# Attention read and rational feed-forward on one core: batch 0's softmax by token halves, early transfers in buffers of the units, and a new list

## The chip, the core and the metric

One core of a Trainium2 chip: TensorE (PE), VectorE (DVE), ScalarE (ACT), GpSimd (POOL), and SyncE (SP), which here issues every DMA. The metric is device microseconds of one execution; lower is better.

## The reference, cut to what matters

Eight batches of eight heads, 512 tokens x and 32 state rows, 64 columns a head.

```python
scores = scale * x @ state.T            # per batch and head
a = softmax(scores, axis=-1)            # "row" softmax, over the 32 states
xread = a @ state
a2 = softmax(scale * state @ x.T, -1)   # "column" softmax, over the 512 tokens
sread = a2 @ x
X = concat([xread, sread], axis=2)      # (B, H, 544, 64) -> rows of 512 = H * D
h = X @ w_in                            # 512 -> 2048
P = a0 + a1*h + a2*h**2 + a3*h**3
Q = 1 + |b0|*|h| + |b1|*h**2
out = (P / (Q + 1e-6)) @ w_out          # 2048 -> 512
```

## The kernel before

**Units.** The hidden width 2048 is cut into U = 8 slices of 256. A unit n is a slice of one batch: n = 8 * batch + slice, 64 units for the token rows; units 64 to 71 do the state reads of all batches. For the token rows `a @ state @ w_in` is regrouped: the products state @ w_in (`extra`, L601, token `X:i` with i = 4 * slice + e; each covers two batches) are made once, in the first 120 us, and are the weights of each unit's first layer. Products of batch 0 are split at once into a high and a low part (`fh` ACT, `fo` DVE); the rest is copied out of PSUM (`XA` by ACT, `XV` by DVE) into a tile `xo` (L618, two buffers), stored to DRAM (`XS`, L624), and loaded and split again later (`lm`, `fs`).

**A unit.** First layer `F:n:0`, `F:n:1` (L696, six matmuls each: high by high, high by low and low by high of the two halves), into a PSUM tile with tag `h`, of which there are two; products, the later batches' scores and transpositions use the same two. Then ACT makes C (`FC`, L708) and A (`FB`, L715) from it; DVE makes three steps that read it, `mu`, `po` on C (L719, L723) and `qd` on A (L729), after which the PSUM buffer is free; ACT `qa`, `ln`, `ex` (a reciprocal through logarithm and exponential, tile L); DVE `g1` (high part of the result, tile gh), `g2`, `g3`; POOL `gl` (low part, tile gl, L759). Second layer `mh:n:t` (four matmuls) and `ml:n:t` (two) for four token tiles t (L769), summed over the eight units of a batch in four PSUM banks, then copied and stored (`fl`/`fv`, `fd`). C and A have three buffers each, L, gh and gl two.

**Weights.** They come as 64-bit words and are converted: a pair k of raw halves is loaded (`lr:2k`, `lr:2k+1`, 512 KB each, L271, tile `raw`, two buffers of two halves); ACT makes one part (`cp`, L294), DVE another (`jr`, L304, "conversion" below), and DVE joins them (`jl`, L320): for input weights into `win_sb` (three buffers, stored by `jw` for later), for output weights into a tile that ACT and POOL split into `wo` (`sp`, L331, L332).

**Batch 0's attention** (L394 to L569). Scores by token halves g (L402), two heads' halves j in two PSUM banks. Row softmax for each j: transposition of blocks of 32 (`row_T`, DVE, L441), maxima (L458), subtraction (L466), exponential (ACT, L490), sums (L494), reciprocal (L500, L501), normalization (L507), transposition back (`a_T`, L513), high part (`a_hi`, ACT, L518), low part (`a_lo`, L522). The first layer of batch 0's units needs the high and low parts of both j. Column softmax: scores copied to SBUF by ACT (`sc_copy`, L412), maximum (`col_max`, DVE, L416) and `col_scale`, exponential with sum (`col_exp`, ACT, L447), transposition by PE (`e2_T`), then the state read (`sread`, L540). Suffixes choose the engine: `row_sub`, `a_lo`, `row_norv` run on DVE, `row_sup`, `a_lp`, `row_norm` on POOL.

**Order.** `ORDER` (L23) is one list of some 2,200 tokens, written out; each token is one call of a function, and each engine runs its instructions in the order of the list. A SyncE transfer that waits for a buffer or for data holds every later one.

```python
    ps_h = ctx.enter_context(tc.tile_pool(name="ps_h", bufs=2, space=PSUM))
    with tc.manual_schedule():
        for name, args in tokens:
            ops[name](*args)
```

Of the kernel before, what the change touches and what calls it, by code (L numbers as in the profile page):

```python
# [9 lines left out]
F32 = mybir.dt.float32  # L10
F32R = mybir.dt.float32r
I32 = mybir.dt.int32
U32 = mybir.dt.uint32
# [5 lines left out]
P = 128  # L19
# [169 lines left out]
def attention_rational_ffn(  # L189
# [7 lines left out]
    nc = tc.nc  # L197
# [10 lines left out]
    CW = DF // U  # L208
# [51 lines left out]
    for u in range(U):  # L260
        groups.append(("out", u))
        if u + 3 < U:
            groups.append(("in", u + 3))
    NU = 2 * len(groups)
    RAW, CV, win_t = {}, {}, {}

    def unit(i):
# [676 lines left out]
```

## Time and profile before

| what | us |
|---|---|
| median of 3 runs (668.93 to 676.08) | 672.35 |
| the profiled execution's own time | 671.54 |
| its span, first to last instruction | 669.7 |
| PE busy | 643.5 |
| DVE busy | 624.2 |
| ACT busy | 515.8 |
| POOL busy | 318.3 |

The span and the busy times are of one profiled execution; what lies around the span is 1.84 us. A busy time counts instructions on the engine, not the queue's waits. Starts are counted from the first instruction.

### The profile page before, as it was taken

Reading aid. Unit: us, or ns where it says so; the run is one execution under the profiler, and the core shown is the slowest. Engines: PE = TensorE matmul, PEld = TensorE weight load, DVE = VectorE, ACT = ScalarE, POOL = GpSimd, SP = SyncE. Lnnn points to the kernel's source line nnn. Section 1 sums busy time; section 2 is a strip of 40 time slices with the busy share of each in tenths; the row PEclk is TensorE's granted clock in tenths of the full one; section 3 lists DMA queues with packets and bytes.
Section 4 is the critical chain, followed back from the end, with each engine's and each line's share of the span. In section 5 each row is a group of like instructions: output and inputs, shape, how many; then the busy total and the mean of one; then the engine's idle time right before and its main releaser. Section 6 shows DMA issues by size and latency. Waiting matters only on the chain.

```text
span 669.7 us, 11219 instructions
## 1 busy us (share of the span) xinstructions
PE 643.5 (96%) x4474; PEld 512.9 (77%) x4474; DVE 624.2 (93%) x593; ACT 515.8 (77%) x611; POOL 318.3 (48%) x172
## 2 busy tenths in 40 slices
PE   6769989999999999999999999999999999999997
PEld 3445556778887888788887888788878888888995
DVE  5889999999999999999999999999999899999885
ACT  4689898887877887787868787797787678865663
POOL 1105255355454566545554545555446446465541
PEclk8989999999999999999999999999999999999999
DMA  7889987615112422213223132231225101211301
GB/s 298 310 315 335 331 329 257 226 54 178 44 34 93 136 77 96 69 26 105 85 101 120 71 89 69 79 142 32 95 79 174 32 1 47 64 47 60 100 1 63
DMA packets 28984, 81.46 MB, mean 122 GB/s; under 512 B 2820, under 2 KB 2948, under 8 KB 28932
## 3 DMA queue, kind: packets, MB, share of 16 engines
q1 hardware_dynamic: 28932, 80.75, 35.1%
q8 instruction: 35, 0.57, 0.3%
q14 instruction: 17, 0.14, 0.1%
HBM read 52.95 MB, written 27.79 MB: 121 GB/s over the span
## 4 chain that ended last, share of the span: by engine, by line
PE 88%; DMA 5%; ACT 3%; DVE 2%; issue 1%; SPq 1%; ACTq 0%
PE h L696 28%; DMA m_dram<-xo 3%; PE ps_x L607 3%; PE o__5754 L769 2%; PE o__3525 L769 2%; PE o__1763 L769 2%; PE o__2310 L769 2%; PE o__4679 L769 2%; PE o__4049 L769 2%; PE o__2879 L769 2%; PE o__3495 L769 2%; PE o__5233 L769 2%; PE o__2341 L769 2%; PE o__5794 L769 2%; PE o__4054 L769 2%; PE o__5172 L769 2%
## 5 line engine op out<-in xcount | busy, mean ns | idle before, releaser
L759 POOL TENSOR_TENSOR gl<-C,L 128x1024 fp32r<-128x1024 f32 (+1 forms) x70 | 174.1, 2487 | 230.4 <-DVE C L752 174.0
L696 PE MATMUL h<-aT,m 128*128 128x512 f32 x768 | 191.3, 396 | 4.2 <-DVE xo L619 4.1
L696 PEld LDWEIGHTS h<-aT,m 128*128 128x128 f32 x768 | 144.9, 190 | 38.5 <-issue 3.5
L708 ACT ACTIVATE C<-h,cst 128x1024 f32<-128x1024 f32 (+1 forms) x72 | 83.3, 1157 | 44.6 <-PE h L696 32.1
L656 POOL TENSOR_TENSOR m<-m_sb,m 128x512 fp32r<-128x512 f32 x56 | 79.9, 1432 | 60.3 <-ACT m L655 40.0
L715 ACT ACTIVATE A<-h,cst 128x1024 f32<-128x1024 f32 (+1 forms) x72 | 76.7, 1066 | 29.2 <-PE h L696 26.9
L740 DVE SCALAR_TENSOR_TENSOR gh<-C,cst,L 128x1024 fp32r<-128x1024 f32 (+1 forms) x72 | 91.8, 1274 | 6.2 <-ACT L L811 2.6
L729 DVE SCALAR_TENSOR_TENSOR A<-A,b0a,h 128x1024 f32<-128x1024 f32 (+1 forms) x72 | 87.5, 1216 | 9.4 <-ACT A L715 7.2
L752 DVE SCALAR_TENSOR_TENSOR C<-C,cst,A 128x1024 f32<-128x1024 f32 (+1 forms) x72 | 88.8, 1233 | 2.2
L723 DVE SCALAR_TENSOR_TENSOR C<-C,cst,h 128x1024 f32<-128x1024 f32 (+1 forms) x72 | 87.8, 1219 | 2.1
L746 DVE SCALAR_TENSOR_TENSOR A<-A,gh 128x1024 f32<-128x1024 f32 (+1 forms) x72 | 88.0, 1222 | 1.6
L735 ACT ACTIVATE A<-A 128x1024 f32<-128x1024 f32 (+1 forms) x72 | 72.7, 1012 | 19.2 <-DVE A L729 19.1
L719 DVE TENSOR_TENSOR C<-C,h 128x1024 f32<-128x1024 f32 (+1 forms) x72 | 82.9, 1152 | 3.9 <-ACT C L708 2.4
L801 ACT ACTIVATE L<-A 128x1024 f32<-128x1024 f32 (+1 forms) x72 | 73.0, 1013 | 3.4 <-POOL gl L759 0.3
L811 ACT ACTIVATE L<-L 128x1024 f32<-128x1024 f32 (+1 forms) x72 | 72.9, 1014 | 1.5
L607 PE MATMUL ps_x<-win_sb,st 64*32 64x256 f32 x1024 | 36.3, 403 | 15.2 <-DVE win_sb L320 6.3
L607 PEld LDWEIGHTS ps_x<-win_sb,st 64*32 64x32 f32 x1024 | 17.8, 111 | 30.9 <-ACT xo L619 10.5
L655 ACT CAST m<-m_sb 128x512 fp32r<-128x512 f32 x56 | 33.9, 614 | 0.0
L619 ACT COPY xo<-ps_x 128x1024 f32<-128x1024 f32 (+1 forms) x26 | 23.8, 933 | 5.0 <-PE ps_x L607 2.8
L332 POOL TENSOR_TENSOR wo<-cv_r,wo 128x1024 fp32r<-128x1024 f32 x7 | 16.9, 2410 | 17.6 <-ACT wo L331 17.6
L696 PEld LDWEIGHTS h<-sh,m 128*128 128x128 f32 x192 | 24.2, 191 | 0.7
L696 PE MATMUL h<-sh,m 128*128 128x256 f32 x192 | 24.4, 283 | 0.0
(254 smaller groups left out, 1113.2 us busy)
## 6 DMA issues: line engine op xcount, KB each, us to landing
m_sb<-m_dram SPq DMA_DIRECT2D x28, 512.0 KB, 4.5
m_dram<-xo SPq DMA_DIRECT2D x24, 512.0 KB, 4.2
out_dram<-o_sb SPq DMA_DIRECT2D x34, 256.0 KB, 4.3
xT_sb<-in_xT_dram SPq DMA_DIRECT2D x16, 512.0 KB, 5.1
raw<-in_w_in_dram SPq DMA_DIRECT2D x16, 512.0 KB, 6.4
raw<-in_w_out_dram SPq DMA_DIRECT2D x16, 512.0 KB, 5.6
x_sb<-in_x_dram SPq DMA_DIRECT2D x16, 512.0 KB, 7.0
w_in_dram<-win_sb SPq DMA_DIRECT2D x8, 512.0 KB, 5.4
```

The lines of the kernel that those rows point to most:

```text
L656: nc.gpsimd.tensor_tensor(m[:, 1], t, m[:, 0].bitcast(F32), op=ALU.subtract)
L696: nc.tensor.matmul(h[:, ci * W : (ci + 1) * W], l, r, start=(q == 0), stop=(q == len(seq) - 1),)
L708: nc.scalar.activation(e["C"], e["h"], AF.Identity, scale=cst[:, 3:4], bias=cst[:, 2:3])
L715: nc.scalar.activation(e["A"], e["h"], AF.Abs, scale=cst[:, 5:6])
L719: nc.vector.tensor_tensor(e["C"], e["C"], e["h"], op=ALU.mult)
L723: nc.vector.scalar_tensor_tensor(e["C"], e["C"], cst[:, 1:2], e["h"], op0=ALU.add, op1=ALU.mult)
L729: nc.vector.scalar_tensor_tensor(e["A"], e["A"], b0a, e["h"], op0=ALU.add, op1=ALU.mult)
L740: nc.vector.scalar_tensor_tensor(e["gh"], e["C"], cst[:, 0:1], e["L"], op0=ALU.add, op1=ALU.mult)
L746: nc.vector.scalar_tensor_tensor(e["A"], e["A"], 1.0 + 1e-6, e["gh"].bitcast(F32), op0=ALU.add, op1=ALU.mult)
L752: nc.vector.scalar_tensor_tensor(e["C"], e["C"], cst[:, 0:1], e["A"], op0=ALU.add, op1=ALU.subtract)
L759: eng.tensor_tensor(e["gl"], e["C"], e["L"], op=ALU.mult)
L769: nc.tensor.matmul(O[t], e[l][:, j * W + t * P : j * W + (t + 1) * P], wo[:, k, 2 * u + j, :], start=(place == FIRST[n // U, t] and i + j ...
```

## The change

1. Row softmax of batch 0 by token halves: `row_T:0:j` takes the 256 tokens of half j from both PSUM banks (two instructions of 128x256), and `a_hi`, `a_lo` write that half of the tokens.
2. Column softmax of batch 0 reads the scores in PSUM; its two `sc_copy` are gone.
3. The raw halves of pairs k = 2, 3 and 4 go to one buffer each of gl, gh and L, tiles of the units that are first written later.
4. The copies of products 0 to 2 go to C buffers, of 3 to 5 to A buffers.
5. In the list: `row_sup` for `row_sub` and `row_norm` for `row_norv` in batch 0, `a_lp` for `a_lo` in batches 0 and 1, `row_sup` for `row_sub` in batch 1, `row_norm:7:0` for `row_norv:7:0`, `gl:69` for `gv:69`; `cp` and `jr` of pairs 2 to 4 by halves; `XV:2`, `XV:26`, `XV:30` for the ACT copies and `XA:4`, `XA:20`, `XA:27` for the DVE ones; the eight warm-up matmuls stand behind the scores; the first stores stand behind ten raw loads; the rest is ordered anew throughout.

```diff
 ORDER = [
-    "warm:8 lt:0:0 ls:0:2 lt:0:1 scores:0:0 lc scores:0:1 cb b0a row_T:0:0 row_max:0:0 row_sub:0:0 lr:1 "
-    "lr:0 cp:0:1 ls:2:8 lr:2 jr:0:1 sc_copy:0:0 cp:0:0 jr:0:0 jl:0 X:0 lr:3 sc_copy:0:1 col_max:0:1 "
-    "col_scale:0:1 row_exp:0:0 row_sum:0:0 row_eps:0:0 cp:1:0 lr:6 XA:0 row_norm:0:0 row_T:0:1 "
-    "row_max:0:1 row_sup:0:1 lr:7 XS:0 fh:0 fo:0 a_T:0:0 X:3 col_exp:0:1 XA:3 X:1 cp:1:1 X:2 "
-    "col_max:0:0 XA:1 XS:3 jr:1:0 jr:1:1 jl:1 X:5 row_exp:0:1 a_hi:0:0 col_scale:0:0 col_exp:0:0 XA:2 "
-    "row_sum:0:1 row_eps:0:1 row_norv:0:1 XS:1 lr:5 lr:4 XS:2 a_T:0:1 a_hi:0:1 a_lp:0:1 a_lo:0:0 lq:0:0 "
...
+    "lt:0:0 ls:0:2 scores:0:0 lt:0:1 row_T:0:0 row_max:0:0 scores:0:1 row_T:0:1 row_sup:0:0 warm:8 "
+    "col_max:0:0 lr:0 cp:0:0 col_scale:0:0 row_max:0:1 lr:1 row_exp:0:0 row_sum:0:0 cp:0:1 row_sup:0:1 "
+    "row_exp:0:1 col_max:0:1 col_scale:0:1 lr:2 cp:1:0 jr:0:1 col_exp:0:0 col_exp:0:1 jr:0:0 jl:0 "
+    "jr:1:0 row_eps:0:0 row_norm:0:0 lc lr:3 cp:1:1 ls:2:8 X:3 lr:7 lr:4 XA:3 X:0 fh:0 jr:1:1 XA:0 X:1 "
+    "row_sum:0:1 row_eps:0:1 row_norm:0:1 lr:8 jl:1 fo:0 lr:6 a_T:0:0 cp:2:0 XA:1 e2_T:0:0 X:5 a_T:0:1 "
+    "a_hi:0:0 a_lp:0:0 lr:5 col_eps:0 cb a_hi:0:1 cp:3:1 cp:3:0 XV:5 lr:11 a_lp:0:1 cp:2:1 b0a XS:0 X:2 "
+    "XV:2 X:4 XA:4 fh:1 jr:2:1 F:0:0 e2_copy:0:0 jr:2:0 jl:2 XS:3 F:0:1 XS:1 cp:4:0 FC:0 fo:1 XS:5 "
+    "F:1:0 jr:4:0 FB:0 jr:3:1 jr:3:0 jl:3 sp:3 qd:0 F:1:1 FC:1 FB:1 mu:0 po:0 qa:0 XS:4 lr:10 ln:0 lr:9 "
+    "cp:4:1 e2_T:0:1 mu:1 po:1 X:8 XA:8 qd:1 fh:2 ex:0 fo:2 XS:2 lq:0:1 jr:4:1 jw:0 jl:4 e2_copy:0:1 "
...
@@ -261,7 +262,13 @@
         groups.append(("out", u))
         if u + 3 < U:
             groups.append(("in", u + 3))
-    NU = 2 * len(groups)
+    EARLY = {2: "gl", 3: "gh", 4: "L"}
+    XEARLY = {0: "C", 1: "C", 2: "C", 3: "A", 4: "A", 5: "A"}
+    BUFS = {"C": 3, "A": 3, "L": 2, "gh": 2, "gl": 2}
+
+    def spare(tag, dtype):
+        return ew.tile([P, 2 * S], dtype, name="spare", tag=tag, bufs=BUFS[tag])
+
     RAW, CV, win_t = {}, {}, {}
 
     def unit(i):
@@ -270,9 +277,13 @@
 
     def load_raw(i):
         what, u, j = unit(i)
-        if i // 2 not in RAW:
-            RAW[i // 2] = cv.tile([P, 2, 2 * CW, 2], U32, name="raw", tag="raw", bufs=2)
-        r = RAW[i // 2][:, j]
+        k = i // 2
+        if k in EARLY:
+            RAW[k, j] = spare(EARLY[k], U32).rearrange("p (f w) -> p f w", w=2)
+        elif (k, 0) not in RAW:
+            t = cv.tile([P, 2, 2 * CW, 2], U32, name="raw", tag="raw", bufs=2)
+            RAW[k, 0], RAW[k, 1], RAW[k, None] = t[:, 0], t[:, 1], t
+        r = RAW[k, j]
         if what == "in":
             nc.sync.dma_start(
                 r.rearrange("p f w -> p (f w)"),
@@ -284,6 +295,11 @@
                 r, w_out[f * P : (f + 1) * P, :].rearrange("p (c w) -> p c w", w=2)
             )
 
+    def raw_words(k, j, w):
+        if j is None:
+            return RAW[k, None][:, :, :, w]
+        return RAW[k, j][:, :, w].unsqueeze(1)
+
     def conv_parts(k, j=None):
         if k not in CV:
             CV[k] = [
@@ -293,7 +309,7 @@
         js = slice(0, 2) if j is None else slice(j, j + 1)
         nc.scalar.activation(
             CV[k][0][:, js].bitcast(F32),
-            RAW[k][:, js, :, 1].bitcast(F32),
+            raw_words(k, j, 1).bitcast(F32),
             AF.Prelu,
             scale=2.0**-112,
             alpha=2.0**32,
@@ -303,7 +319,7 @@
         js = slice(0, 2) if j is None else slice(j, j + 1)
         nc.vector.tensor_scalar(
             CV[k][1][:, js],
-            RAW[k][:, js, :, 0],
+            raw_words(k, j, 0),
             2.0**-29,
             7.0,
             op0=ALU.mult,
@@ -415,7 +431,7 @@
         cm = once(b, "cm", at_tile("cm", [P, 2], 2))
         nc.vector.tensor_reduce(
             cm if j is None else cm[:, j : j + 1],
-            half(TS[b]["sT"], j),
+            half(TS[b].get("sT", TS[b]["ps"]), j),
             axis=AX.X,
             op=ALU.max,
         )
@@ -437,8 +453,14 @@
 
     def row_T(b, j=None):
         e1 = once(b, "e1", at_tile("e1", [P, 2, S]))
-        for i in (0, 1) if b == 0 and j is None else (j,):
-            nc.vector.transpose(flat(half(e1, i)), flat(half(TS[b]["ps"], i)))
+        if b:
+            nc.vector.transpose(flat(e1), flat(TS[b]["ps"]))
+            return
+        w = S // 2
+        for i in range(2):
+            nc.vector.transpose(
+                e1[:, j, i * w : (i + 1) * w], half(TS[b]["ps"], i)[:, j * w : (j + 1) * w]
+            )
 
     def col_exp(b, j):
         T = TS[b]
@@ -446,7 +468,7 @@
         r2 = once(b, "r2", at_tile("r2", [P, 2], 2))
         nc.scalar.activation(
             e2[:, j],
-            T["sT"][:, j],
+            half(T.get("sT", T["ps"]), j),
             AF.Exp,
             scale=SCALE,
             bias=T["cm"][:, j : j + 1],
@@ -512,17 +534,27 @@
         t = once(b, "eT", lambda: at.tile([P, 2, S], F32, name="eT", tag="e2" if b else "e2T"))
         nc.vector.transpose(flat(half(t, j)), flat(half(TS[b]["e1"], j)))
 
+    def halves(b, t, j):
+        if b:
+            return half(t, j)
+        w = S // 2
+        return t[:, :, j * w : (j + 1) * w]
+
+    def turned(b, j):
+        t = half(TS[b]["eT"], j)
+        return t if b else t.rearrange("p (j t) -> p j t", j=2)
+
     def a_hi(b, j=None, copy=None):
         if b not in AT:
             AT[b] = at.tile([P, 2, 2, S], F32R, name="aT", tag="aT", bufs=2)
-        (copy or nc.scalar.copy)(half(AT[b][:, 0], j), half(TS[b]["eT"], j))
+        (copy or nc.scalar.copy)(halves(b, AT[b][:, 0], j), turned(b, j))
 
     def a_lo(b, j=None, eng=None):
         a = AT[b]
         (eng or nc.vector).tensor_tensor(
-            half(a[:, 1], j),
-            half(TS[b]["eT"], j),
-            half(a[:, 0].bitcast(F32), j),
+            halves(b, a[:, 1], j),
+            turned(b, j),
+            halves(b, a[:, 0].bitcast(F32), j),
             op=ALU.subtract,
         )
 
@@ -615,7 +647,11 @@
     def extra_out(i, copy):
         u, e = divmod(i, B // 2)
         q0 = 1 if e == 0 else 0
-        t = XO[i] = ew.tile([P, 2, 2, CW], F32, name="xo", tag="xo", bufs=2)
+        if i in XEARLY:
+            t = spare(XEARLY[i], F32).rearrange("p (q j f) -> p q j f", q=2, j=2)
+        else:
+            t = ew.tile([P, 2, 2, CW], F32, name="xo", tag="xo", bufs=2)
+        XO[i] = t
         copy(t[:, q0:].rearrange("p q j f -> p j q f"), XP[i][:, :, q0:])
 
     def extra_store(i):
```

## Rows read from the trace of the kernel before

**Rows 1.** The page: the span, the busy time of each engine with its share of the span and its instructions, and of the 40 equal slices those of PE and of the DMA engines (tenths; a slice is 16.7 us).

```profile
span 669.7 us, 11219 instructions
...
PE 643.5 (96%) x4474; PEld 512.9 (77%) x4474; DVE 624.2 (93%) x593; ACT 515.8 (77%) x611; POOL 318.3 (48%) x172
...
PE   6769989999999999999999999999999999999997
...
DMA  7889987615112422213223132231225101211301
```

**Rows 2.** Four stretches of the span: from:to and length in us, then the busy us of PE, PEld, DVE, ACT and POOL, each with its instructions, PE's granted clock, the busy share of the DMA engines and GB/s.

```profile
0.00:50.00 50.00, 33.30 (x483) 21.59 (x484) 36.98 (x52) 33.39 (x47) 7.23 (x11) 0.86 0.86 308
50.00:120.00 70.00, 64.95 (x913) 43.13 (x912) 66.46 (x66) 62.78 (x72) 32.60 (x14) 1.00 0.85 312
120.00:660.00 540.00, 540.00 (x3061) 444.55 (x3060) 517.60 (x472) 418.49 (x491) 278.08 (x148) 1.00 0.25 81
660.00:669.70 9.70, 5.22 (x22) 3.68 (x21) 3.20 (x5) 1.17 (x2) 0.40 (x1) 0.96 0.19 54
```

**Rows 3.** Stretches of 2 us in the first 50 us, the same columns (the clock of a stretch is 1.00 at 2.4 GHz and 0.50 at 1.2 GHz).

```profile
8.00:10.00 2.00, 0.00 (x0) 0.00 (x0) 1.93 (x4) 1.86 (x6) 0.00 (x0) 1.00 1.03 416
10.00:12.00 2.00, 0.16 (x8) 0.16 (x16) 1.88 (x4) 1.41 (x4) 0.00 (x0) 0.54 1.04 401
...
26.00:28.00 2.00, 0.61 (x3) 0.19 (x1) 0.37 (x2) 0.74 (x1) 0.00 (x0) 1.00 1.04 424
...
32.00:34.00 2.00, 2.00 (x5) 0.99 (x3) 2.00 (x3) 0.00 (x0) 1.87 (x1) 0.50 0.89 266
```

**Rows 4.** TensorE's matmuls in order of time: start us, us, engine, line, operation, out<-in, count, and in brackets how long PE had been idle and what released it. The first three rows are of 0 to 40 us (the rows of one start stand by instruction), the rest of 20 to 125 us.

```profile
5.54 0.63 PE L402 MATMUL ps_sc__110<-xT_sb,st 64*32 64x256 f32 x1
...
6.85 0.40 PE L402 MATMUL ps_sc__109<-xT_sb,st 64*32 64x256 f32 x1 [0.67 <-DMA xT_sb<-in_xT_dram]
...
11.84 3.67 PE L607 MATMUL ps_x<-win_sb,st 64*32 64x256 f32 x64 [4.01 <-DVE win_sb L320]
...
23.57 3.04 PE L696 MATMUL h<-aT,m 128*128 128x512 f32 x12 [1.18 <-DVE xo L619]
29.51 4.49 PE L696 MATMUL h<-aT,m 128*128 128x512 f32 x12 [2.90 <-DVE xo L619]
...
44.76 4.37 PE L696 MATMUL h<-aT,m 128*128 128x512 f32 x12
...
50.88 1.09 PE L607 MATMUL ps_x<-win_sb,st 64*32 64x256 f32 x32
...
78.25 1.10 PE L607 MATMUL ps_x<-win_sb,st 64*32 64x256 f32 x32 [0.93 <-ACT xo L619]
```

**Rows 5.** VectorE in order of time, the same columns.

```profile
7.60 0.72 DVE L441 STREAM_TRANSPOSE e<-ps_sc__109 128x512 f32<-128x512 f32 x1 [6.62 <-PE ps_sc__110 L402]
...
10.56 1.23 DVE L320 SCALAR_TENSOR_TENSOR win_sb<-cv_y,cv_r 128x1024 int32<-128x1024 int32 x1
...
23.44 0.92 DVE L304 TENSOR_SCALAR cv_r<-raw 128x1024 int32<-128x1024 uint32 x1
...
28.67 0.69 DVE L619 COPY xo<-ps_x 128x512 f32<-128x512 f32 x1 [2.30 <-DMA m_dram<-xo]
...
36.28 1.28 DVE L729 SCALAR_TENSOR_TENSOR A<-A,b0a,h 128x1024 f32<-128x1024 f32 x1 [1.48 <-ACT A L715]
...
48.99 0.68 DVE L619 COPY xo<-ps_x 128x512 f32<-128x512 f32 x1
```

**Rows 6.** What SyncE's queue of DMA issues waited for up to 125 us: line, releaser, us in total, times, longest.

```profile
SPq L624 <- ACT xo L619: 57.3, 22, 6.2
```

**Rows 7.** Groups of instructions in 0 to 70 us, one row for each shape: line, engine, operation, out<-in, shapes, count, then busy us, mean ns, and the idle time before them.

```profile
L619 ACT COPY xo<-ps_x 128x1024 f32<-128x1024 f32 x10 | 10.0, 1013 | 0.8 <-PE ps_x L607 0.5 <-DMA m_dram<-xo 0.3
...
L304 DVE TENSOR_SCALAR cv_r<-raw 128x1024 int32<-128x1024 uint32 x7 | 5.0, 719 | 0.0
L719 DVE TENSOR_TENSOR C<-C,h 128x1024 f32<-128x1024 f32 x4 | 4.9, 1214 | 0.0
L708 ACT ACTIVATE C<-h,cst 128x1024 f32<-128x1024 f32 x4 | 4.8, 1205 | 3.4 <-PE h L696 3.4
...
L636 DVE TENSOR_TENSOR m<-ps_x,m 128x512 fp32r<-128x512 f32 x4 | 2.7, 686 | 0.1
L294 ACT ACTIVATE cv_y<-raw 128x512 f32<-128x512 f32 x4 | 2.7, 673 | 0.7 <-DMA raw<-in_w_in_dram 0.6
...
L304 DVE TENSOR_SCALAR cv_r<-raw 128x512 int32<-128x512 uint32 x4 | 1.5, 420 | 0.0
...
L458 DVE TENSOR_REDUCE mx<-e 128x16 f32<-128x512 f32 x2 | 1.4, 686 | 0.1
L494 DVE TENSOR_REDUCE rs<-e 128x16 f32<-128x512 f32 x2 | 1.4, 682 | 0.2 <-ACT e L490 0.2
L416 DVE TENSOR_REDUCE cm<-sT 128x1 f32<-128x512 f32 x2 | 1.3, 662 | 0.0
...
L522 POOL TENSOR_TENSOR aT<-eT,aT 128x512 fp32r<-128x512 f32 x1 | 1.3, 1272 | 6.5 <-ACT aT L518 6.5
...
L466 POOL TENSOR_TENSOR e<-e,mx 128x512 f32<-128x512 f32 x1 | 1.1, 1051 | 0.2 <-DVE mx L458 0.2
...
L522 DVE TENSOR_TENSOR aT<-eT,aT 128x512 fp32r<-128x512 f32 x1 | 0.6, 649 | 0.0
```

306 rows, old and new, of the table ORDER are left out of this document.

## The prediction

> **What bounds the kernel now.** I read the page first, then stretches of the span, then TensorE's and VectorE's instructions in order of time. The page has PE busy for 643.5 of 669.7 us and DVE for 624.2 [rows 1]; the slices show that PE is short of full only in the first seven and the last. The stretches put numbers on it [rows 2]: from 120 to 660 us PE has no idle time. Its 26.2 us of idle time are 50 - 33.30 = 16.7 us before 50 us, 70 - 64.95 = 5.05 us from 50 to 120 us, and 9.70 - 5.22 = 4.5 us at the end. All matmuls of the changed kernel are those of before, so it can only win idle time, and what PE loses at 1.2 GHz.
>
> In the first 50 us the reader is to see three things. (a) PE waits for conversions and for PSUM buffers that nobody has emptied: the first products start at 11.84 us, after 4.01 us of idle time, released by the first joined weights; the first layers of units 0 and 1 start at 23.57 and 29.51 us, each released by DVE's copy of a product [rows 4]. (b) That copy at 28.67 us had itself waited 2.30 us for a store of products, which held its buffer [rows 5]: a buffer of two, emptied through a queue in which SyncE waited 57.3 us for ACT's copies up to 125 us [rows 6]. (c) After long idle times the granted clock falls to 0.50 (32 to 34 us; 0.54 already at 10 to 12 us) [rows 3]: the 12 matmuls of a unit's first layer take 3.04 us at full clock, and 4.49 and 4.37 us in the two that were hit [rows 4]. From some 30 us on DVE's own work sets the pace: up to the end of the copy at 48.99 us it was busy for 36.98 us [rows 2, 5].
>
> **The change, part by part.** Times are of the profiled execution, 671.54 us (span 669.7 plus 1.84 around it). The median of the three runs is 672.35, 0.8 us more, and the runs spread over 7 us.
>
> *Row softmax by token halves, column softmax from PSUM.* A half now needs only the scores of its own 256 tokens. Those of the first half end at 6.17 us (5.54 + 0.63); the second half's start at 6.85 [rows 4]. So DVE's first transposition starts at 6.3 instead of 7.60 us [rows 5]. It is now two instructions of 128x256, which the trace doesn't show: between half of 0.72 us and 0.72 us each [rows 5], so 0.72 to 1.43 us a half; I take 0.8, near the half, since all DVE rows here scale with elements. The column maximum reads PSUM: 0.66 us from SBUF [rows 7]; the bounds are 0.6 and 0.72, the transposition that reads PSUM, and I take 0.66. ACT loses two copies, which is nothing on the path.
> But DVE now does more ahead of the first weights: 0.8 + 0.69 (maxima) + 0.2 (the second half's scores end at 7.95 if PE is still at 1.2 GHz, since the warm-up matmuls moved behind them) + 0.8 + 0.66 + 0.15 + 0.69 + 0.68 + 0.66 + 0.15, then two halves of 0.42 and the join of 1.23 [rows 5, 7]: from 6.3 to 13.7 us. The first product starts 1.9 us later than the 11.84 of before. The weights aren't what is late then: at 400 GB/s and over [rows 3] the first two raw halves are there by some 9.5 us.
>
> *Raw weights and products in the units' buffers.* Ten raw loads now stand ahead of the first store on SyncE's queue, and nine of them (4.7 MB) wait for no buffer; the tenth waits for unit 0's raw halves, read at 12.6 us. With the inputs ahead of them that is 6.8 MB by 20 us at 400 GB/s; nothing below needs one earlier than it lands. The first six products go to buffers of their own, so no copy waits for a store. In exchange the first C and A of units 0 and 1 wait for those stores, which now lie behind the loads: the first would land at some 22.5 us and the fourth at 26.5, and C and A of unit 0 are due at 25.9 and 27.1. Hidden by 3 us; at the 300 GB/s of the first 50 us [rows 2] it would cost up to 2 us.
>
> Now the walk. Products 3 and 0 from 13.7: 1.83 us each at half clock as before (3.67 for two [rows 4]), or 1.09 each; I take half clock. ACT's split of product 0 ends at 17.8; DVE meanwhile does both halves' rest and the join of weights 1 to 17.2, the low part 0.69 to 18.6, two transpositions and the copy of product 5 to 21.1, and the copy of product 2 (1.21) to 22.3. That frees the PSUM buffer of unit 0's first layer: 22.3 against 23.57. POOL's two low parts (1.27 each [rows 7]) follow ACT's casts at 20.6 and 21.4 and end at 23.2; so the layer ends at 25.9 and not 25.4. Unit 1's layer follows at once, since its inputs were ready at 25.0, and ends at 28.9 at full clock; before it ended at 34.0. **The lead is 5.1 us there.** From here DVE leads: its three steps on each of units 0 and 1 from 28.2 (two activations of ACT, 1.2 and 1.1 [rows 7], after 25.9) to 35.5, then low part 0.69, half 0.42, join 1.2, two steps of unit 0 2.4, conversion 0.72, join 1.2, third step 1.2, low part 0.69 and copy 0.69, to 44.7, when product 13 can start. Before, it started at 50.88 with one group of four output matmuls (0.93 us) more behind it: **a lead of 5.2 us**. DVE's sum agrees: the 36.98 us less the steps that are moved to POOL (0.69 + 0.69 + 0.65) and 0.16, plus 0.52 for product 2 being a whole copy and 0.1 for halves, is 35.4; begun at 6.3 that ends at 41.7 with no wait, and the walk has 3 us of waits, where before had 7.6 ahead of the first and 5 after it.
>
> *Warm-up matmuls, constants.* Moved behind the scores, no instruction more. If they hold the clock up, products 3 and 0 save 2 x 0.74 us and the lead is 6.3; the walk has 5.2. I take 5.5.
>
> *Work moved to POOL.* Five steps of batches 0 and 1. POOL takes 1.05 us for what DVE did in 0.69, and 1.27 for 0.65 [rows 5, 7]; batch 0's chains have that room except for the 0.5 us counted above. What is queued behind is in POOL's order the first unit's last step, which is due at 43. A DVE conversion beside POOL's low part took 0.92 us (at 23.44) where the group's mean is 0.72 [rows 5, 7], so 0.2 a meeting, three of them, 0.6 us, within the choice above.
> [...]
>
> *The list from 50 us on.* PE's 5.05 us of idle time from 50 to 120 us are waits for ACT's copies of products, such as the 0.93 at 78.25 us [rows 2, 4]. The new list has the same pairs of products behind each other, and batch 1 gives DVE 2.6 us of work less; I take 0.5 us of gain in a range of -3 to +3, and let it be eaten by the meetings with POOL. From 120 to 660 us nothing, as PE has nothing to win there; at the end the order behind the last first layer has the same matmuls: 0, within 1.
>
> Sum: 671.54 - 5.5 = 666.0; half of the 0.8 between this execution and the median goes on top: **666.4 us**, with 663.5 to 669 as its own range.
>
> **Rivals.** *More than the lead.* If DVE's relief also clears the waits from 50 to 120 us (5.05 down to 2) and no first layer meets the low clock (1.45 and 1.33 us of before, of which the walk has one left), the gain is 6.3 + 3 = 9.3: 662 us. For it: DVE had just 70 - 66.46 = 3.5 us of idle time there [rows 2], so less work counts. Against it: the waits named are ACT's.
>
> *The lead is given back.* Up to 120 us the DMA engines are busy for 0.85 of the time [rows 2]; the same bytes have to be through 5.5 us earlier, and stores and raw loads now share buffers. If the queue holds the third and fourth pair of weights back, PE waits again between 50 and 100 us; 1 to 2 us are left: 670.5. For it: SyncE's waits [rows 6]. Against it: a share of 0.85 leaves room for 5%.
>
> *Slower: a gap in the full stage.* The list is new over all of 540 us. DVE is busy there for 517.6 of 540 [rows 2]; a step placed too early in it holds DVE behind a PE result, and PE's two PSUM buffers pass that on. One gap of 2 us in each of seven batches is 14 us against 5.5: 680 us. It decides where DVE's slack, 22 us over the stage, is spent in one place in each batch; a wait of over 2 us ahead of DVE's step on A (L729), batch after batch, would show it. Against it: the old list had the same tightness with no gap.
>
> **How the numbers follow.** Forecast 0.52, more gain 0.20, given back 0.21, slower 0.07. A difference of 1% is 6.7 us, about what a measurement of this kernel can tell from no change: below 665.6 lie all of "more" and some 0.21 of the forecast's 0.52, so faster 0.41; slower (over 679) 0.04; within 0.55. The range leaves a tenth at either end: 660 to 673.
>
> **What would show it.** First join ends near 13.7 us (later than before), and no copy of a product waits for a store before 40 us; unit 1's first layer ends near 29 us; product 13 starts near 45; PE's idle time before 50 us falls from 16.7 to some 12 us, from 50 to 120 us it stays at 4 to 6. Wrong: unit 1's first layer later than 32 us, activations of units 0 and 1 released by stores, or PE under 10.00 in any stretch of 10 us between 120 and 650 us.

## The result, and the profile of the changed kernel

The changed kernel takes 675.75 us (median of 11 runs, 674.18 to 678.38), the kernel before 671.99 in the same series (11 runs, 668.93 to 676.08): a ratio of 1.0063 with an interval of 1.0039 to 1.0086. It is slower by 0.6%, some 3.8 us. The forecast was 666.4, and 675.75 lies outside its range of 660 to 673. The profiled execution took 678.32 us (span 676.5), the second longest of the 11.

The page of the changed kernel, the same lines as [rows 1]:

```profile
span 676.5 us, 11211 instructions
...
PE 645.3 (95%) x4474; PEld 511.7 (76%) x4474; DVE 629.3 (93%) x591; ACT 513.9 (76%) x612; POOL 317.8 (47%) x179
...
PE   4788999899999999999999999999999999999997
```

Its stretches, as [rows 2]:

```profile
0.00:50.00 50.00, 33.93 (x522) 21.72 (x522) 38.02 (x56) 34.46 (x49) 14.63 (x15) 0.90 0.84 316
50.00:120.00 70.00, 64.24 (x858) 43.06 (x861) 66.55 (x64) 60.13 (x69) 28.81 (x14) 0.98 0.82 303
120.00:660.00 540.00, 535.21 (x3055) 437.64 (x3048) 515.19 (x460) 414.12 (x487) 271.79 (x149) 1.00 0.25 81
660.00:676.50 16.50, 11.91 (x54) 9.29 (x53) 9.55 (x14) 5.16 (x9) 2.59 (x2) 1.00 0.11 32
```

The reader is to see two surprises. PE's idle time before 50 us fell by 0.6 us only, to 16.07. And the stage from 120 to 660 us, where PE had no idle time in [rows 2], has 540 - 535.21 = 4.79 us. DVE is busier by 5.1 us although the change takes steps away from it: it is held for longer (below).

**The front does what was worked out, some 2 us late.** PE, the answers to [rows 4]:

```profile
8.02 0.60 PE L418 MATMUL ps_sc__98<-xT_sb,st 64*32 64x256 f32 x1 [1.95 <-DMA xT_sb<-in_xT_dram]
...
14.79 4.33 PE L639 MATMUL ps_x<-win_sb,st 64*32 64x256 f32 x96 [2.72 <-DVE win_sb L336]
...
24.14 5.73 PE L732 MATMUL h<-aT,m 128*128 128x512 f32 x24 [0.33 <-ACT cv_y L310]
...
33.30 1.10 PE L639 MATMUL ps_x<-win_sb,st 64*32 64x256 f32 x32 [2.99 <-DVE C L759]
36.94 5.19 PE L639 MATMUL ps_x<-win_sb,st 64*32 64x256 f32 x96 [2.54 <-DVE A L765]
...
46.94 1.09 PE L639 MATMUL ps_x<-win_sb,st 64*32 64x256 f32 x32
```

DVE, the answers to [rows 5]:

```profile
6.15 0.45 DVE L461 STREAM_TRANSPOSE e<-ps_sc__98 128x256 f32<-128x256 f32 x1 [5.17 <-PE ps_sc__99 L418]
...
9.20 0.45 DVE L461 STREAM_TRANSPOSE e<-ps_sc__98 128x256 f32<-128x256 f32 x1 [1.56 <-PE ps_sc__99 L418]
...
13.51 1.22 DVE L336 SCALAR_TENSOR_TENSOR win_sb<-cv_y,cv_r 128x1024 int32<-128x1024 int32 x1
...
21.43 2.56 DVE L655 COPY spare<-ps_x 128x1024 f32<-128x1024 f32 x2
```

The first layers of units 0 and 1 run in one go and end at 29.87 us (before: 34.0). No copy up to 45 us waits for a store. The granted clock is 0.63 at 14 to 16 us and 0.52 at 16 to 18, behind PE's 2.72 us of idle time, and the first three products took 4.33 us. From here on the text uses a lead, an estimate from two traces: PE's matmul work done by a given time, each matmul counted at the mean spacing of its shape at full clock, less that of the kernel before at the same time. It is 2.8 us at 47 us and 3.5 at 60.

**Then the lead goes.** It is +0.4 us at 64 us, -0.2 at 69, +1.1 at 118, -0.9 at 128 and up to 236, -2.2 at 263, -4.2 at 345, -5.9 at 560 and -6.7 at 641. The places show in two fences. POOL, five steps that start within 0.4 us of a DVE step, one that comes after it (255.50) and one beside a DVE step of another kind (333.40):

```profile
57.48 2.40 POOL L348 TENSOR_TENSOR wo<-cv_r,wo 128x1024 fp32r<-128x1024 f32 x1 [6.74 <-ACT wo L347]
...
78.50 2.41 POOL L348 TENSOR_TENSOR wo<-cv_r,wo 128x1024 fp32r<-128x1024 f32 x1 [5.24 <-ACT wo L347]
...
236.45 2.40 POOL L795 TENSOR_TENSOR gl<-C,L 128x1024 fp32r<-128x1024 f32 x1 [4.96 <-PE o__2372 L805]
...
255.50 3.41 POOL L795 TENSOR_TENSOR gl<-C,L 128x1024 fp32r<-128x1024 f32 x1 [4.27 <-DVE C L788]
...
333.40 1.30 POOL L692 TENSOR_TENSOR m<-m_sb,m 128x512 fp32r<-128x512 f32 x1
334.66 2.39 POOL L554 TENSOR_TENSOR aT<-eT,aT 128x1024 fp32r<-128x1024 f32 x1
...
551.39 2.39 POOL L795 TENSOR_TENSOR gl<-C,L 128x1024 fp32r<-128x1024 f32 x1 [3.83 <-DVE C L788]
```

DVE at the same places:

```profile
57.51 3.46 DVE L788 SCALAR_TENSOR_TENSOR C<-C,cst,A 128x1024 f32<-128x1024 f32 x1
...
78.56 3.43 DVE L782 SCALAR_TENSOR_TENSOR A<-A,gh 128x1024 f32<-128x1024 f32 x1
...
236.43 3.50 DVE L776 SCALAR_TENSOR_TENSOR gh<-C,cst,L 128x1024 fp32r<-128x1024 f32 x1
...
255.35 1.28 DVE L776 SCALAR_TENSOR_TENSOR gh<-C,cst,L 128x1024 fp32r<-128x1024 f32 x1
...
333.38 1.24 DVE L759 SCALAR_TENSOR_TENSOR C<-C,cst,h 128x1024 f32<-128x1024 f32 x1
334.75 3.38 DVE L776 SCALAR_TENSOR_TENSOR gh<-C,cst,L 128x1024 fp32r<-128x1024 f32 x1
...
551.78 3.08 DVE L776 SCALAR_TENSOR_TENSOR gh<-C,cst,L 128x1024 fp32r<-128x1024 f32 x1 [0.56 <-PE o__4626 L805]
```

Read start and end together. A DVE step with both inputs in SBUF takes 1.28 us (1.22 for L782); where POOL began ahead of it or within 0.02 us of it, it ends 1.08 or 1.09 us after POOL does (236.45 + 2.40 + 1.08 = 239.93). So 1.08 of its 1.28 us lie behind POOL's end. Such a pair is called a meeting here, and the DVE step is held. At 255 us the order is reversed: DVE keeps its 1.28 us and POOL takes 3.41 instead of 2.40. A DVE step with one input in PSUM wasn't held: L759 kept 1.24 us at 333.38, while POOL ran from 333.40 to 334.70. In the traces of the two kernels 348 such steps of 128x1024 have POOL running beside them for over 0.6 us, and none took more than 1.28 us. Summed over the span, the unit's steps with two inputs in SBUF (L776, L782, L788) take 17.1 us more than at the median of their shape; in the kernel before (L740, L746, L752) it is 9.0, with four holds of 1.0 to 1.1 us as its longest, such as this one:

```profile
196.51 2.36 DVE L740 SCALAR_TENSOR_TENSOR gh<-C,cst,L 128x1024 fp32r<-128x1024 f32 x1
```

PE's idle places: one behind the meeting at 57 us, and those from 120 us on:

```profile
62.15 1.91 PE L639 MATMUL ps_x<-win_sb,st 64*32 64x256 f32 x32 [1.95 <-DVE xo L655]
...
125.11 3.02 PE L732 MATMUL h<-aT,m 128*128 128x512 f32 x12 [1.39 <-ACT xo L655]
...
246.21 0.74 PE L805 MATMUL o__2316<-wo,gl 128*128 128x512 f32 x2 [0.82 <-POOL gl L795]
...
340.73 1.63 PE L732 MATMUL h<-aT,m 128*128 128x512 f32 x6 [1.34 <-DVE r L497]
...
554.91 1.20 PE L805 MATMUL o__4717<-wo,gh 128*128 128x512 f32 x4 [0.97 <-DVE gh L776]
```

The last three lie 10, 6 and 3 us behind a held step. These three gaps are 3.13 of the 4.79 us. That at 125 us, 1.39 us, is another matter: ACT's copy of a product at 124.04 had waited 1.69 us for the store that frees its buffer.

### The profile page after: what moved, and what is told of

Its sections match the earlier page's. It is cut to its first block, busy times and chain, and to the rows that moved or that the text cites. A ratio compares the mean times of both kernels' runs of the same rounds, so it can differ in the third digit from the quotient of the medians.

```text
span 676.5 us, 11211 instructions
## 1 busy us (share of the span) xinstructions
PE 645.3 (95%) x4474; PEld 511.7 (76%) x4474; DVE 629.3 (93%) x591; ACT 513.9 (76%) x612; POOL 317.8 (47%) x179
## 4 chain that ended last, share of the span: by engine, by line
PE 84%; DVE 8%; issue 2%; ACT 2%; DMA 2%; POOL 1%; SPq 0%; DVEq 0%; POOLq 0%; ACTq 0%
PE h L732 28%; PE ps_x L639 3%; PE o__4717 L805 2%; PE o__3487 L805 2%; PE o__5760 L805 2%; PE o__4626 L805 2%; PE o__5202 L805 2%; PE o__5235 L805 2%; PE o__1758 L805 2%; PE o__3479 L805 2%; PE o__3472 L805 2%; PE o__4053 L805 2%; PE o__5786 L805 2%; PE o__5254 L805 2%; PE o__5215 L805 2%
## 5 line engine op out<-in xcount | busy, mean ns | idle before, releaser
L795 POOL TENSOR_TENSOR gl<-C,L 128x1024 fp32r<-128x1024 f32 (+1 forms) x71 | 167.7, 2362 | 278.7 <-DVE C L788 183.4
L732 PE MATMUL h<-aT,m 128*128 128x512 f32 x768 | 188.4, 392 | 3.5 <-ACT xo L655 1.7
L732 PEld LDWEIGHTS h<-aT,m 128*128 128x128 f32 x768 | 142.9, 188 | 37.9 <-ACT xo L655 4.7
L776 DVE SCALAR_TENSOR_TENSOR gh<-C,cst,L 128x1024 fp32r<-128x1024 f32 (+1 forms) x72 | 98.5, 1367 | 7.9 <-ACT L L847 3.4
L788 DVE SCALAR_TENSOR_TENSOR C<-C,cst,A 128x1024 f32<-128x1024 f32 (+1 forms) x72 | 91.2, 1267 | 2.1
L759 DVE SCALAR_TENSOR_TENSOR C<-C,cst,h 128x1024 f32<-128x1024 f32 (+1 forms) x72 | 87.8, 1220 | 2.1
L782 DVE SCALAR_TENSOR_TENSOR A<-A,gh 128x1024 f32<-128x1024 f32 (+1 forms) x72 | 87.0, 1211 | 1.9
L692 POOL TENSOR_TENSOR m<-m_sb,m 128x512 fp32r<-128x512 f32 x56 | 76.4, 1372 | 26.1 <-ACT m L691 20.3
L639 PE MATMUL ps_x<-win_sb,st 64*32 64x256 f32 x1024 | 37.9, 424 | 12.8 <-DVE C L759 3.0
L655 ACT COPY xo<-ps_x 128x1024 f32<-128x1024 f32 (+1 forms) x22 | 20.0, 916 | 7.6 <-PE ps_x L639 2.9
```

The source lines that it names most:

```text
L639: nc.tensor.matmul(ps[k * NS : (k + 1) * NS, j, q, :], st[j * D : (j + 1) * D, 2 * e + q, k, :], win_t[u][j * D : (j + 1) * D, k, :], star ...
L732: nc.tensor.matmul(h[:, ci * W : (ci + 1) * W], l, r, start=(q == 0), stop=(q == len(seq) - 1),)
L759: nc.vector.scalar_tensor_tensor(e["C"], e["C"], cst[:, 1:2], e["h"], op0=ALU.add, op1=ALU.mult)
L776: nc.vector.scalar_tensor_tensor(e["gh"], e["C"], cst[:, 0:1], e["L"], op0=ALU.add, op1=ALU.mult)
L782: nc.vector.scalar_tensor_tensor(e["A"], e["A"], 1.0 + 1e-6, e["gh"].bitcast(F32), op0=ALU.add, op1=ALU.mult)
L788: nc.vector.scalar_tensor_tensor(e["C"], e["C"], cst[:, 0:1], e["A"], op0=ALU.add, op1=ALU.subtract)
```

## The experiments

Times of before differ by series; the ratio is always to the kernel before on the same chip.

**1 to 4: where in the list the loss lies.** The list was cut and joined: new up to product 13, then old (e1); new up to unit 8's first layer at 125 us, then old (e2); old up to there, with the old code, then new (e3). In e4 the whole list is new, but two splits of output weights on POOL come later:

```
e1  ... sread:0:0 sread:0:1 XS:9 cp:7 lr:13 jr:7 jl:7 X:13
-   ml:0:2 mh:0:3 ml:0:3 X:7 XS:12 XA:13 ...
+   lt:1:1 col_norm:0 lr:12 sr_copy:0 ln:1 mh:0:3 XA:13 ...
e2  ... F:8:0 fs:9 jw:6 jl:15 sp:15 mu:7 po:7 F:8:1
-   FB:8 ml:5:0 mh:5:3 qd:7 ...
+   ml:5:0 mh:5:1 mh:6:1 ml:5:3 qd:7 ...
e3  ... F:7:0 g1:6 g2:6 g3:6 F:8:1 mh:5:1 sv:14 F:8:0
-   cp:15 FC:7 mh:6:1 ml:5:3 FB:7 ...
+   ml:5:2 cp:15 jr:15 FB:7 gl:6 ...
e4
-   sp:7 FB:3 FC:3 ... g3:1 gl:1 XV:11 ... g2:3 sp:9 ...
+   FB:3 FC:3 ... g3:1 gl:1 sp:7 XV:11 ... gl:3 sp:9 ...
```

> The changed kernel with its list up to product 13 (47 us in its trace), and behind that the rest of the old list in the old order. Theory A (the new front is ahead by 3 us at 47 us, and the rest of the new list loses it again, mostly by DVE steps that are held while POOL runs): ahead of the kernel before by about 3 us, some 669 us, if the old rest opens no gap of its own; DVE instructions held for 2 us or more should then be rare. Theory B (the new front itself is what costs, by its buffers, its loads ahead of the stores or the clock): as slow as the changed kernel, 676 us.

> The changed kernel with its list up to the first layer of unit 8 (some 125 us), and behind that the rest of the old list. Theory A: what the changed kernel loses before 120 us stays (it is 1.9 us behind there by the matmul work that remains), the 4.8 us of PE idle time from 120 to 660 us go: some 672 to 674 us. If the gaps of the full stage cost nothing in the time, it stays at 676.

> The kernel before with its old list up to the first layer of unit 8, and behind that the rest of the new list. Theory A: the new rest costs by its gaps, +2 to +5 us on the kernel before, 674 to 677, if DVE and POOL meet as in the changed kernel; the same time as the kernel before if the meetings depend on the phase that the front leaves. Theory B: the same time as before, 672.

> The changed kernel, with the split of two pairs of output weights (the ACT cast and the POOL subtraction of pairs 7 and 9) one place later in the list, behind the low parts of units 1 and 3; PE's, DVE's and SyncE's order stay. In the changed kernel each of these two POOL subtractions starts 0.03 to 0.06 us ahead of a DVE step with two SBUF inputs, which then takes 3.46 and 3.43 us where 1.28 and 1.22 are usual. Theory A: both are gone, PE's idle 1.95 us at 62 us and the low clock behind it too, 3 to 5 us less: 671 to 673 us. Theory B: no change, 676 us.

Measured, against 670.80 of before: e1 673.66 (1.0036, 1.0020 to 1.0053); e2 672.24 (1.0019, 1.0001 to 1.0037); e3 680.17 (1.0130, 1.0105 to 1.0155); e4 676.10 (1.0066, 1.0045 to 1.0088). e1 was a poor cut: at its seam PE waits for work that the new front doesn't do first, and that alone takes the lead:

```profile
52.65 2.08 PE L804 MATMUL o__632<-wo,gh 128*128 128x512 f32 x4 [4.61 <-ACT sr L583]
```

It stands for neither theory. e2 and e3 do tell: the front without the rest of the list is within 0.4% of before, and the rest without the front is 1.3% slower, with the same three holds and gaps (holds at 238.1, 336.4 and 553.5 us). So the rest loses. e3 lost more than the 674 to 677 us expected: by the lead, some 3.6 us of its loss lie between 130 and 200 us, behind its own seam, and 5.7 from 236 to 641 us. e4 took both early meetings away (held time 12.8 us in place of 17.1) and gained nothing. Its lead was 3.9 us at 96 us, 2.6 at 98, where PE waited 1.58 us for POOL's `gl`, and 0.6 at 128; e9, e10, e14 and e15 below have the same gap at 98 us.

**5 and 6: the three late meetings.** e5 leaves out the three POOL steps: units 18 and 54 use their gh where gl belongs, batch 4 its high part where the low part belongs. e6 leaves nothing out and lets DVE do them:

```
e5, in fourth(n, eng)
+        if n in (18, 54):
+            e["gl"] = e["gh"]
+            return
...
e5, in a_lo(b, j, eng)
+        if b == 4:
+            return
...
e6, in the list
- gl:18  gl:54  a_lp:4
+ gv:18  gv:54  a_lo:4
```

> The changed kernel without three POOL instructions, those that in its trace start within 0.4 us of a DVE step with two inputs in SBUF: the fourth step of units 18 and 54 (L795; their second layer reads gh in its place) and the low part of batch 4's weights (L554; its products read the high part in its place). Nothing is put on another engine. Theory L (these meetings hold DVE by 2.2, 2.1 and 1.8 us and PE's gaps of 0.82, 1.34 and 0.97 us some 4 to 10 us later are their price): the three gaps go, PE idles under 2 us between 120 and 660 us where it idled 4.79, and the time is 675.7 - 3.1 = 672.6 us, down to 671.5. Rival S (the new list has no slack at those places, with or without the meetings): at least two of the gaps stay, and the time is 675 to 676.

> The changed kernel with the same three steps done by DVE in place of POOL, at the same places of the list; nothing is left out. DVE gets 3 x 1.2 us of work and loses 2.2 + 2.1 + 1.8 us of held time, so it is ahead by some 0.9, 0.9 and 0.6 us at each place. Theory L: part of each gap goes, PE idle between 120 and 660 us about 2.5 to 3.5, the time 673.5 to 674.5 us. Rival S: 675 to 677.

e5: 674.09 us (1.0046, 1.0025 to 1.0068); e6: 672.45 (1.0012, 0.9992 to 1.0033); before 671.38. e6 took 3.3 us away by the medians (3.4 by the ratios) where 1.3 to 2.3 were expected, and the intervals of the two ratios don't overlap. PE's stage is full again but for 0.57 us; 1.4 of the 4.2 us between this and the changed kernel's row belong to the wait at 125 us, which this execution doesn't have (see e10):

```profile
120.00:660.00 540.00, 539.43 (x3022) 441.89 (x3007) 517.34 (x471) 416.24 (x489) 268.95 (x148) 1.00 0.24 80
```

e5 lost the three gaps as well, but got two others. DVE in e5, then PE:

```profile
252.12 2.93 DVE L779 SCALAR_TENSOR_TENSOR gh<-C,cst,L 128x1024 fp32r<-128x1024 f32 x1 [0.70 <-ACT L L853]
...
560.71 1.28 DVE L779 SCALAR_TENSOR_TENSOR gh<-C,cst,L 128x1024 fp32r<-128x1024 f32 x1 [2.46 <-PE o__4670 L811]
```

```profile
255.10 1.19 PE L811 MATMUL o__2316<-wo,gh 128*128 128x512 f32 x4 [0.90 <-DVE gh L779]
...
565.91 1.62 PE L735 MATMUL h<-aT,m 128*128 128x512 f32 x3 [2.07 <-DVE C L762]
```

One is a new meeting (POOL's fourth step began at 251.56), which the moved timing made. The other is of the experiment's own making: unit 54's gh is now held until its last product, and a later step on gh waits 2.46 us for it. Each gap follows a held or waiting DVE step, so by the gaps S is out. By its time e5 fits neither forecast: 674.09 us lies between 672.6 and 675, and PE idles 3.82 us from 120 to 660 where under 2 were expected. What carries theory L is e6, and e9 and e10 below, which don't have the three gaps either. None of these runs keeps the three steps on POOL and moves only their start; that the hold is what delays PE is read from the rows of DVE. Here a change that freed DVE moved the later steps, so meetings were exchanged, not only removed (2.93 us at 252.12).

**7 and 8: are the first 130 us bound by bytes?** The eight stores of first-layer weights are left out of either kernel; the last units load x in place of what was stored.

```
     def store_win(u):
-        nc.sync.dma_start(w_in32[u], win_t[u])
+        pass
...
-        nc.sync.dma_start(t, w_in32[n % U])
+        nc.sync.dma_start(t, xT[n % U, 0])
```

> The changed kernel without the eight stores of first-layer weights (512 KB each, six of them before 135 us: 3.1 MB, at the 300 to 330 GB/s of the first 120 us some 9.5 us of DMA time); the loads of the last units read x in their place, as many bytes. Theory B2 (bytes pace the first 130 us in both kernels, so the lead of 3 to 4 us that the new front has up to 118 us can't last): without the stores the lead at 130 us is +2 or more over the kernel before where it was -1, and the time is 672.5 us or less; the kernel before without its stores gains as well, 2 us or more. Rival O (the waits at 118 to 128 us come from the order of the queue alone): the lead at 130 us is -1 to 0, the time 675 to 676, and the kernel before gains nothing.

> The kernel before without the same eight stores (the last units' loads read x in their place). Theory B2: PE idle in the first 120 us falls from 21.7 us by 2 or more, the time is 668.5 us or less. Rival O: 670 to 671 us.

e7: 674.92 us (1.0062, 1.0042 to 1.0082); e8: 670.72 (1.0001, 0.9982 to 1.0019). The kernel before gains nothing from 4 MB less, and its idle time up to 120 us stays (16.63 + 5.46). In e7 the gap at 125 us is gone and the lead at 128 us is +0.9, between the two expectations; the time moved by 0.8 us, which the intervals don't separate from nothing. That the stores made the gap isn't shown, since e6's profiled execution has them and lacks the gap too. The bytes of these stores do not set the time of either kernel.

**9 to 11.** e9 is e6 with e4's two moves; e10 is e9 with the store of first-layer weights 6 behind the next load of products. e11 undoes one part of the change:

```
e10
- FC:7 F:8:0 fs:9 jw:6 ... mu:8 lm:10 fs:10 ...
+ FC:7 F:8:0 fs:9 ... mu:8 lm:10 jw:6 fs:10 ...
e11
-    XEARLY = {0: "C", 1: "C", 2: "C", 3: "A", 4: "A", 5: "A"}
+    XEARLY = {}
```

> The changed kernel with the three steps on DVE of the run before last (672.45 us alone) and the splits of output weights 7 and 9 two and some tokens later on POOL, as in the earlier run where these took the meetings at 57 and 78 us away (nothing gained alone: 676.1). If the time of PE up to 130 us counts in full once the later gaps are gone: the lead over the kernel before is 3 us or more at 98 us, half of it is left at 128 us, and the time is 670 to 671.3 us, under 672.45. If the wait for the copies of the last products at 118 to 128 us gives all of it back whatever was gained before: 672 to 673 us.

> As e9_five_moved, and one transfer moved: the store of first-layer weights 6 (512 KB, issued at 120.7 us in the changed kernel while the store that frees a product's buffer takes 5 us to land) stands behind the next load of products in SP's queue, some 5 us later. If that transfer's share of the DMA engines is what lengthens the wait of ACT's copy at 122 to 124 us: the gap of PE at 122 to 125 us (0.96 to 1.39 us) goes, the lead at 128 us is 3 us, and the time is 1 to 1.5 us under e9_five_moved. If the order of the two product buffers alone sets it: the gap stays and the times are equal.

> The changed kernel without one part of the change: the first six state products are copied into the two xo buffers again, not into buffers of the units. This prices that part. In the kernel before, the waits that end with these copies and their stores were some 10 us of PE's waiting in the first 50 us; if the buffers are what lets the products run, product 13 comes 2 to 4 us later than the 46.9 us of the changed kernel. If a lead of the front reaches the end, the time is 677.5 to 680 us; if it is given back at 118 to 128 us as in the runs so far, it is 675 to 677 us.

e9: 672.35 us (1.0016, 1.0002 to 1.0030); e10: 672.59 (1.0008, 0.9989 to 1.0027); before 671.44. Neither gains on e6 (672.45). The stretch from 118 to 130 us, in the changed kernel and then in e9:

```profile
118.00:130.00 12.00, 10.27 (x186) 7.13 (x171) 9.33 (x9) 9.12 (x12) 4.37 (x3) 1.00 0.85 288
```

```profile
118.00:130.00 12.00, 10.28 (x159) 7.43 (x148) 8.92 (x9) 9.19 (x13) 4.39 (x3) 1.00 0.92 309
```

PE loses 1.7 us in both, with and without the early meetings, and 1.3 in e10 (a gap of 1.10). One store's place isn't its cause. But it is no fixed price of the list. Up to 236 us e6 has the list of the changed kernel, and its profiled execution (670.58 us, its second shortest) lost 0.1 us in this stretch, less than the kernel before (11.77 busy):

```profile
118.00:130.00 12.00, 11.89 (x101) 8.74 (x82) 11.31 (x10) 10.42 (x12) 7.23 (x4) 1.00 0.78 265
```

The meeting at 57 us is missing there as well. DVE's step began 0.09 us ahead of POOL's, where in the changed kernel it began 0.03 us behind, and POOL was the one held. DVE, then POOL:

```profile
56.89 1.28 DVE L788 SCALAR_TENSOR_TENSOR C<-C,cst,A 128x1024 f32<-128x1024 f32 x1
```

```profile
56.98 3.42 POOL L348 TENSOR_TENSOR wo<-cv_r,wo 128x1024 fp32r<-128x1024 f32 x1 [7.01 <-ACT wo L347]
```

So the front's loss differs from execution to execution of one list. e6's lead was 3.3 us from 130 to 236 us. Then it fell to 1.0 at 641, though the three gaps are gone; e9's fell from 0.2 to -2.2, e10's from 0.9 to -1.4. Only some 0.55 us of these 2.3 show as idle time of PE. With the old rest (e2, e14) the lead doesn't move from 150 us on.

e11: 683.17 us (1.0155, 1.0131 to 1.0179), slower than the changed kernel by 7.4 us (medians; 6.2 by the ratios); 675 to 680 was expected, by either theory too little. Its ACT and its DVE show what the part of the change does:

```profile
22.77 1.01 ACT L655 COPY xo<-ps_x 128x1024 f32<-128x1024 f32 x1 [4.36 <-DMA m_dram<-xo]
29.66 0.59 ACT L655 COPY xo<-ps_x 128x512 f32<-128x512 f32 x1 [2.98 <-DMA m_dram<-xo]
```

```profile
23.98 1.23 DVE L655 COPY xo<-ps_x 128x1024 f32<-128x1024 f32 x1 [4.17 <-DMA m_dram<-xo]
28.46 1.23 DVE L655 COPY xo<-ps_x 128x1024 f32<-128x1024 f32 x1 [3.26 <-DMA m_dram<-xo]
```

Product 13 starts at 54.49 us, 7.55 later than in the changed kernel, and most of it is still there at the end: what the front loses here is kept.

**12 to 15: two products later, and the front alone again.** e12 is e9, and e13 is e2, with products 29 and 31 behind unit 7's first layer; e14 and e15 are e2 and e13 with the two splits later.

```
- X:29 g1:6 g2:6 ... XA:29 X:31 ... F:7:1 fs:8 F:7:0 XA:31 FB:7 ... mh:6:3 FC:7
+ g1:6 g2:6 ... F:7:1 fs:8 F:7:0 X:29 XA:29 FB:7 ... mh:6:3 X:31 FC:7 XA:31
```

> As e9_five_moved (672.35 us), with the last two state products (29 and 31) and their copies behind unit 7's first layer and unit 6's second layer in the list, where they stood ahead of them. In e9_five_moved ACT's copy of product 29 waited 1.49 us for the store that frees its buffer and PE waited 1.16 us behind that copy, at 122.9 to 124.0 us. If the place of these two products in the order is what gives the front's lead back: the gap goes, the lead over the kernel before at 128 us is 1.2 to 2.5 us where it was -0.6, and the time is 670 to 671.3 us. If something else holds that stretch (bytes, or units 7 and 8 wait for their folded weights anyway): PE idles elsewhere between 118 and 135 us by the same 1 us and the time is 672 to 673 us.

> As e2_front_125 (the new front up to 125 us, then the list of before; 672.24 us), with the same two products later. There the gap was 0.96 us at 122 us and a second one of 1.25 us stood at 141 us, behind the seam. If the order of the two products gives the lead back: the first gap goes, the time is 670.8 to 671.5 us. If not: 672 to 673 us.

> e2_front_125 (672.24 us) with the splits of output weights 7 and 9 later on POOL, behind the fourth steps of units 1 and 3. If the two early meetings, which come in some executions and not in others, are what the front loses: no run over 673 us, the median 670 to 671 us, 0.2% faster than the kernel before. If the front's lead is lost at 118 to 128 us whatever comes ahead of it: 672 to 673 us, no difference from e2_front_125.

> e13_front_products (673.13 us, 669.4 to 675.5) with the same two splits later. If the meetings make the spread: 669.5 to 671 us, and no run over 673. If the stretch from 118 to 128 us makes it: 672 to 673.5 us.

e12: 675.47 us (1.0050, 1.0032 to 1.0068); e13: 673.13 (1.0016, 0.9995 to 1.0038), both against 672.08 of before; e14: 671.35 (1.0004, 0.9989 to 1.0020); e15: 672.38 (1.0024, 1.0010 to 1.0038), against 671.02. e12 is a miss in the other direction. Its PE waits longer, one unit later:

```profile
126.78 3.54 PE L732 MATMUL h<-aT,m 128*128 128x512 f32 x9 [1.91 <-ACT xo L655]
```

The wait moves along with the copies. e14 ties with the kernel before: its highest run is 673.13 us (e2: 674.05) and its median 0.35 us above the 670 to 671 that was expected if the early meetings make the loss; the interval overlaps that of e2. e15's interval overlaps that of e13 too. These meetings alone were not what the front lacks. But e2 and e14 aren't the front alone: both pay for their seam, where e2's lead falls from 2.3 us at 137 us to 0.6 at 142, and e14's from 1.6 to 0.2. In e2:

```profile
140.85 1.10 PE L417 MATMUL ps_sc<-xT_sb,st 64*32 64x256 f32 x32 [1.25 <-issue]
```

e13 doesn't have this gap and kept a lead of 2.2 us to the end in its profiled execution (669.36 us, its shortest), but its runs reach 675.53. No version here beats the kernel before.

## Why the prediction was wrong

**The walk up to 47 us: right in kind, 2.2 us too early.** First join 14.7 instead of 13.7 us: the second half's scores started at 8.02, not 6.85, so DVE waited 1.56 us. First layers to 29.87 instead of 28.9, without the low clock. Product 13 at 46.94 instead of 44.7: PE waited 2.99 and 2.54 us for DVE at 33 and 37 us. The lead was 2.8 us at 47 us, where 5.5 was taken. The sum of DVE's steps was right: 35.2 us of work up to the end of the copy at 46.46 us, where 35.4 was worked out. The waits were mis-sized: some 5 us in place of 3, 1.56 of them for the second half's scores ("end at 7.95", measured 9.12, behind a later DMA) and 1.45 for ACT's copy of a product (L655) at 19.48. The warm-up matmuls did not hold the clock up either (0.63 at 14 to 16 us, 0.52 at 16 to 18), which was counted on in part. The clock is read here as a share of full speed, which is all that the traces give. Two of its sums are slightly off: its own terms put the first join at 13.85, not 13.7, and 5.2 plus 2 x 0.74 is 6.7, not 6.3; neither carries the miss. That the products' own buffers carry the front is shown by e11 (6.2 to 7.4 us).

**The step that failed first: "0.2 a meeting".** The price came from one row in [rows 5], a DVE conversion of 0.92 us beside POOL. That row is of another kind of step, with one input in SBUF. For a step with both inputs in SBUF a meeting cost what POOL had left to run, less 0.2 us: 2.2, 2.1 and 1.8 us for the three late ones, from POOL's 2.4. The traces tell the two kinds apart: beside POOL, L776 took 3.38 us at 334.75, where 1.28 is usual, and L759, with one input in PSUM, 1.24 at 333.38. The kernel before shows the hold already (2.36 us for L740 at 196.51), so its rows were enough to search the new list for POOL steps that come free just as a step on gh, A or C starts. The prediction counted three meetings, 0.6 us in all, by that one row.

**The step that cost most: "from 120 to 660 us nothing, as PE has nothing to win there".** It was read from a full stage that a full stage stays full. PE lost 4.79 us there, 3.13 of them in three gaps behind meetings and 1.39 in the wait at 125 us. Putting three steps on DVE took 3.3 of the 3.8 us away (e6), though it gives DVE 3 x 1.2 us more work. By the lead the changed kernel's profiled execution loses 5.8 us between 236 and 641 us, where nothing was forecast; 2.3 of them stay in e6, e9 and e10 without the three meetings, and their cause is open. The rival "a gap in the full stage" was right in kind and put at 0.07. It was wrong in its place (three in the whole stage, not one in each batch), its size (4.8 us, not 14) and its trigger: POOL, not a step placed too early behind a PE result. Its test, a stretch of 10 us with PE under 10.00, is met.

**"The lead is given back".** This rival came true in part: at 57.51 us one meeting held the third step, the DVE copy behind it came late, and PE lost 1.95 us and then had a granted clock of 0.57 from 62 to 66 us. With the early meetings gone (e4, e9) the lead was 3.7 to 3.9 us at 96 us, and was given back at 98 us (a wait for POOL's `gl`) and from 118 to 128 us, behind ACT's copies of the last products. In e6's profiled execution it was not given back by 236 us. The mechanism that the rival named, the bytes of the queue, is not seen: e7 and e8 gained nothing without 4 MB of them.

**What stays open.** First, why most profiled executions with the new front lose 1 to 2.6 us of PE at 118 to 130 us. It is a wait of ACT's copies for a store of products to free a buffer (1.69 us in the changed kernel, at 124.04). The gap was absent in e7, without the stores of weights, and in e6, with them; moving one store didn't take it away, and moving the two products moved it. A third buffer would test it directly and wasn't tried. Second, where the rest of the new list loses its other 2.3 us from 236 to 641 us. What the front alone is worth isn't shown: the joined lists show no gain that can be measured (e14, 0.9989 to 1.0020), with a seam of their own in e2 and e14, though a front made worse is paid nearly in full (e11).

## What to carry to other kernels

Where DVE and POOL both work all the time, price each new order by its meetings: list the DVE steps with two SBUF inputs, and ask of each which POOL instruction can start just ahead of it; here the price was POOL's remaining time less 0.2 us, not an average, and a shift of 0.1 us decided which of the two paid. Two engines that shared a step cost less here with the slow one's part done by the fast one at that place (some 1.2 us on DVE, 1.24 for L554, against 2.1 us of holding). A stage in which the bound engine has no idle time says that the old order has no gap; it says nothing about a new order.

## What was not expected of the hardware

Who is held was decided within some 0.02 us. At 236.43 us DVE's row begins 0.02 us ahead of POOL's and DVE was the one held, at this place in all five traces that have it; in e7 a lead of 0.04 us (57.70 against 57.74) was enough to hold POOL, which took 3.49 us, and no DVE step of this kind with a lead of 0.04 us or more was held for over 0.3 us in any of the 17 traces. So one list can have a meeting in one execution and not in the next. Of the units' 128x1024 steps 126 are held for over 0.3 us in these traces, and all end 1.08 or 1.09 us behind POOL, so such a row is best read by its end. That a held step's row begins at its issue, not where its data starts to move, is the author's reading; no row shows it.
